# The softmax of q without GpSimd: exp with bias and sum on ScalarE head by head, the product on VectorE, and six kinds of subtractions and additions moved to VectorE

## The chip, the core and the metric

The kernel runs on one core of a Trainium2 chip. The metric is the device time of one execution in microseconds (us); the median of three runs stands below. Engines go by the names of the profile: PE (TensorE's matmuls), PEld (its weight loads, which overlap), DVE (VectorE), ACT (ScalarE), POOL (GpSimd), SP (SyncE, which issues most DMAs). "PEclk" is the granted clock of TensorE as a share of 2.4 GHz; its lower level is 1.2 GHz.

## The reference, cut to what matters

All data are fp32. The softmax of q runs over the 64 values of one head; that of k runs over the sequence.

```python
# q, k, v: (8 batches, 8 heads, 576 positions, 64)
q_s = exp(q - max(q, axis=-1));  q_s = q_s / (sum(q_s, axis=-1) + 1e-9)
k_s = exp(k - max(k, axis=2));   k_s = k_s / (sum(k_s, axis=2) + 1e-9)
kv = einsum("bhsd,bhse->bhde", k_s, v)
x = einsum("bhsd,bhde->bhse", q_s, kv)        # -> x: (4608 tokens, 512)

xn = x / sqrt(mean(x * x, axis=-1) + 1e-6) * rms_g          # first MoE
g = xn @ w_gate                                             # 512 -> 1536
x = (g * sigmoid(g) * (xn @ w_val)) @ w_out                 # 1536 -> 512

h = maximum(maximum(x @ w1, x @ w2), x @ w3)                # second MoE, 512 -> 768
out = h @ w_out2                                            # 768 -> 512
```

## The kernel before

**Tiles.** The 4608 tokens make nine groups of 512 (`g` 0 to 8); the last one gathers the last 64 positions of each batch. Each group has four pairs of heads `p`, of 128 features. A tile of q, `q_t[g, p]`, has 128 partitions (positions) and 512 columns: 8 pieces of 64, four blocks of positions times two heads, and each piece is one row of the softmax. The text calls such a piece of 64 columns a head, as the code does. An fp32 product is made of high and low halves in a reduced format: three matmuls, high by high, high by low and low by high. So every operand is split by a cast (the high half) and a subtraction (the low half).

**Stages.** (1) The prologue makes group 0's attention and joins the first weights out of 64-bit words (table `stages`). (2) Groups 0, 1 and 2 run as singles: `iteration(g, nxt, f)` for 12 hidden blocks `f`. Each makes the gate product pg (12 matmuls), tanh, product pv (12), the hidden block in halves hh and hl, and `out1` for the block before (12). In group 0, the weights of the next blocks are joined beside it (`scale` on ACT, `join` L164 to L166 on DVE, `high` on ACT, `low` L183 with half 0 on POOL and half 1 on DVE), and the attention of group 1 is made. (3) Groups 3 to 8 run in pairs (3+4, 5+6, 7+8), with quarter products whose sums replace some matmuls. (4) The second MoE runs over all groups.

**Attention beside a single.** From group 1 on, every engine but SP keeps the order in which the program is written (`tc.manual_schedule`); before that, the scheduler decides it. `beside_single` calls `attend(g, n, part, ...)` at fixed places of each iteration. Step n of group g does: `q_divide(g, n-1)` (part 0, at the head of the iteration), `make_kv(n-1)` (part 1), `transpose_q(n-1)`, `k_max(n)`, `q_exp(n)` and a load (part 2, between products pg and pv), `make_x(n-1)` (part 4), the exp of k (parts 5 and 6). Steps 5 and 6 make the variance, three Newton steps for the reciprocal root, and the normalised x. Group 1 carries the attention of group 3 (from f=0) and of group 2 (from f=5), group 2 that of group 4. In the pairs 3+4 and 5+6 the same `attend` serves the next two groups.

**Softmax of q.** `q_exp`: maximum on DVE (L346), subtraction on POOL (L347), one exp of 128x512 on ACT (L348). `q_divide`, an iteration later: sum on DVE (L352), addition of a small constant (L353), reciprocal (L355), product on POOL (L356). `transpose_q` follows: four PE transposes of the result (L401) into bank `pt`.

**Other work on POOL.** `Sums.whole` (L287) adds both halves of the first weights again, w = wh + wl, two additions every second iteration of groups 1 and 2; DVE makes four quarter sums of w (L292 to L295). Each of those is then split: cast on ACT (L259), subtraction on POOL (L260), store by SP (L261): one quarter in the even iteration, three in the odd one. `make_x` ends with the square of x on ACT (L444) and its addition to `sacc` on POOL (L445). POOL also makes hl (L830) in groups 0 and 1, the low halves of group 0's raw x (`split_first`, L455), and half of the shared splits of the first operands of the pairs in group 2 (L739).

Of the kernel before, what the change touches and what calls it, by code (L numbers as in the profile page):

```python
# [8 lines left out]
F32 = mybir.dt.float32  # L9
F32R = mybir.dt.float32r  # L10
I32 = mybir.dt.int32
AF = mybir.ActivationFunctionType
ALU = mybir.AluOpType
# [37 lines left out]
def attention_moe_moe(ctx: ExitStack, tc: tile.TileContext, q, k, kt, v, w1, rms_g, w2, w2_out, out):  # L51
# [81 lines left out]
    class Weights:  # L133
# [45 lines left out]
        def low(self, f, h):  # L179

            hi = wh[1, f].rearrange("p j n -> p (j n)")[:, h * HALF : (h + 1) * HALF]
            engine = nc.gpsimd if h == 0 else nc.vector
            engine.tensor_sub(self.half(1, f, h), self.y.pop((f, h)), hi.bitcast(F32))  # L183

    class Ahead:

# [94 lines left out]
    class Sums:  # L281


        def whole(self, f):
            st = two.tile([P, 2, N], F32, tag="st", name=f"w1_{f}")
            for j in range(2):
                nc.gpsimd.tensor_add(st[:, j, :], wh[1, f][:, j, :].bitcast(F32), wl[1, f][:, j, :].bitcast(F32))  # L287
            a, b = slice(0, N // 2), slice(N // 2, N)
            a11, a12, a21, a22 = st[:, 0, a], st[:, 0, b], st[:, 1, a], st[:, 1, b]
            q = two.tile([P, 4, N // 2], F32, tag="st", name=f"q1_{f}")  # L290
            self.q = {n: q[:, i, :] for i, n in enumerate((S1, S2, S4, S3))}
            nc.vector.tensor_add(self.q[S1], a21, a22)  # L292
            nc.vector.tensor_sub(self.q[S2], self.q[S1], a11)
            nc.vector.tensor_sub(self.q[S4], a12, self.q[S2])
            nc.vector.tensor_sub(self.q[S3], a11, a21)  # L295
# [45 lines left out]
                nc.sync.dma_start(t, kv_dram[p, :, 4 * i : 4 * i + 4, :])  # L341
                kv8[p].append(t)

    def q_exp(g, p):
        qm = two.tile([P, 24], F32, tag="qm", name=f"qm_{g}_{p}")[:, 0:8]
        nc.vector.tensor_reduce(qm, q_t[g, p], axis=AX.X, op=ALU.max)  # L346
        nc.gpsimd.tensor_sub(q_t[g, p], q_t[g, p], qm.unsqueeze(2).to_broadcast([P, 8, 64]))  # L347
        nc.scalar.activation(q_t[g, p], q_t[g, p], AF.Exp)  # L348

    def q_divide(g, p):  # L350
        qs = two.tile([P, 8], F32, tag="qs", name=f"qs_{g}_{p}")
        nc.vector.tensor_reduce(qs, q_t[g, p], axis=AX.X, op=ALU.add)  # L352
        nc.vector.tensor_scalar(qs, qs, EPS_SM, None, op0=ALU.add)  # L353
        qr = two.tile([P, 8], F32, tag="qr", name=f"qr_{g}_{p}")
        nc.vector.reciprocal(qr, qs)  # L355
        nc.gpsimd.tensor_mul(q_t[g, p], q_t[g, p], qr.unsqueeze(2).to_broadcast([P, 8, 64]))  # L356

    def k_max(g, p):
        if g == NB:
# [57 lines left out]
    def make_x(g, p):  # L417
        px = pair_bank(g, p, "px", "a0")
        if g == NB:
            for b in range(NB):  # L420
                s = slice(64 * b, 64 * b + 64)
                nc.tensor.matmul(px[:, s], kv8[p][b // 4][:, b % 4, :], qrt[g, p][:, s], start=True, stop=True)
        elif g in WHOLE:
            nc.tensor.matmul(px, kv_raw[p % 2], qrt[g, p], start=True, stop=True)
        else:
            nc.tensor.matmul(px, kvh[g, p], qh[g, p], start=True, stop=False)
            nc.tensor.matmul(px, kvh[g, p], ql[g, p], start=False, stop=False)
            nc.tensor.matmul(px, kvl[g, p], qh[g, p], start=False, stop=True)
        xraw[g, p] = one.tile([P, N], F32, tag=f"xraw{p}", name=f"xraw_{g}_{p}")
        if g == 0:  # L430
            if p in (0, 3):
                sqs["t", p] = wpool.tile([P, 3, N], F32, tag="wl4" if p == 0 else "wh4", name=f"sqs_{p}")
            sqs[p] = sqs["t", 0][:, p, :] if p < 3 else sqs["t", 3][:, 0, :]
            nc.scalar.activation(xraw[g, p], px, AF.Copy, scale=gain[:, p : p + 1])
            split_first(p)
            nc.scalar.activation(sqs[p], px, AF.Square)
            return
        nc.scalar.copy(xraw[g, p], px)
        if p == 0:
            sacc[g] = one.tile([P, N], F32, tag="sacc", name=f"sacc_{g}")  # L440
            nc.scalar.activation(sacc[g], xraw[g, p], AF.Square)
        else:
            sq = two.tile([P, N], F32, tag="y", name=f"sq_{g}_{p}", bufs=3)
            nc.scalar.activation(sq, xraw[g, p], AF.Square)  # L444
            nc.gpsimd.tensor_add(sacc[g], sacc[g], sq)  # L445

    xh, xl = {}, {}
    rawh, rawl = {}, {}
# [1 line left out]
    def split_first(p):  # L450

        b = wpool.tile([P, 2, N], F32R, tag=("wh11", "wl11", "wl6", "wl9")[p], name=f"raws_{p}")
        rawh[p], rawl[p] = b[:, 0, :], b[:, 1, :]
        nc.scalar.copy(rawh[p], xraw[0, p])
        nc.gpsimd.tensor_sub(rawl[p], xraw[0, p], rawh[p].bitcast(F32))  # L455

    def sum_squares(g, p):
        if p == 0:
# [78 lines left out]
    def attend(g, n, part, done=lambda p: None):  # L537

        before = 1 <= n <= 4
        if part == 0 and before:  # L540
            q_divide(g, n - 1)
        elif part == 1 and before:
            make_kv(g, n - 1)
        elif part == 2 and n <= 4:
            if before:
                transpose_q(g, n - 1)
            if n < 4:
                k_max(g, n)
                q_exp(g, n)
            if n < 3:  # L550
                load_pair(g, n + 1)
        elif part == 4 and before:
            make_x(g, n - 1)
        elif part == 5 and n < 4:
            k_exp(g, n, False)
        elif part == 5 and n == 4:
            split_squares(g)
        elif part == 3 and n == 5:
            variance(g)
        elif part in (4, 5) and n == 5:  # L560
            newton_step(g, part - 4)
        elif part == 0 and n == 6:
            newton_step(g, 2)
        elif part == 2 and n == 6:
            for p in range(4):
                done(p)
        elif part == 6 and n < 4 and g < NB:
            nc.scalar.activation(k_t[g, n], k_t[g, n], AF.Exp)
# [103 lines left out]
    def plane(n):  # L672

        if n // 3 not in kept:
            tag = f"w{'hl'[n // 3 % 2]}{4 + n // 6}"
            kept[n // 3] = wpool.tile([P, 3, N], F32R, tag=tag, name=f"x_{tag}")
        return kept[n // 3][:, n % 3, :]
# [56 lines left out]
    def split_operand(which, shared=False):  # L734
        for kk in range(2):
            n = 4 * which + 2 * kk
            if shared and kk == 1:
                nc.scalar.copy(plane(n), operand(which, kk))
                nc.gpsimd.tensor_sub(plane(n + 1), operand(which, kk), plane(n).bitcast(F32))  # L739
            else:  # L740
                split(plane(n), plane(n + 1), operand(which, kk))

# [17 lines left out]
    def iteration(g, nxt, f):  # L760
# [66 lines left out]
        if ahead:  # L827
            first.low(f + 1, 0)
            first.high(f + 1, 1)
        (nc.gpsimd if ahead or g == 1 else nc.vector).tensor_sub(hl[g, f], t, hh[g, f].bitcast(F32))  # L830
        if nxt is not None and f == 9 and nxt not in COMPACT:
            split_squares(nxt)
        if f > 0:
# [391 lines left out]
```

## Time and profile before

| what | value |
|---|---|
| median of three runs | 1672.43 us (1671.51 to 1672.44) |
| the profiled execution | 1672.9 us |
| its span in the trace | 1671.1 us |
| mean granted clock | 0.965 |
| busy: PE, DVE, ACT, POOL | 1534.3, 1002.7, 579.5, 473.8 us |

The span is the time from the first to the last instruction that the trace shows; the time of the execution has 1.8 us around it. Busy shares are means over stages that differ, so stages are read one by one: the prologue up to 59.5 us, group 0 up to 180.4, group 1 up to 363.3, group 2 up to 502.4, the pairs up to 1140, and then the second MoE.

### The profile page before, as it was taken

The page shows a single profiled execution, that of the slowest core. Times are in us where ns is not written, and L with a number is a line of the kernel's source. Part 1 is how long each engine was busy: PE and PEld are TensorE (multiplying, and loading weights), DVE is VectorE, ACT ScalarE, POOL GpSimd, SP SyncE. Part 2 cuts the span into 40 slices and gives each one's busy share as a digit, 9 for nine tenths or more (in the row PEclk, how much of TensorE's full clock was granted, in tenths as well). Part 3 has the DMA queues.
Part 4 walks back from the last instruction along what each step waited for, and adds up shares of the span by engine and source line. Part 5 has one row for each costly group of instructions (what it writes and reads, how often), then busy time and mean ns, then how long its engine had stood idle before and what let it go on. Part 6 is the DMA issues. An engine that isn't in the chain of part 4 may idle for free.

```text
span 1671.1 us, 19265 instructions
## 1 busy us (share of the span) xinstructions
PE 1534.3 (92%) x6734; PEld 1242.2 (74%) x6734; DVE 1002.7 (60%) x1581; ACT 579.5 (35%) x1033; POOL 473.8 (28%) x471
## 2 busy tenths in 40 slices
PE   5788876787899989999899999999999999999999
PEld 4576755565777767777787888888888888888887
DVE  6999434454477778768877566655364554544501
ACT  4544322333335434444343433432141231322211
POOL 4454243443354434224353132301100101101000
PEclk8899987988999999999999999999999999999999
DMA  7667532325416867687675978788454454544441
GB/s 253 261 219 266 197 112 97 107 69 181 162 70 235 306 218 244 223 321 262 211 255 189 346 281 274 240 276 319 143 191 167 168 194 170 181 159 170 153 145 45
DMA packets 136816, 337.61 MB, mean 202 GB/s; under 512 B 13328, under 2 KB 50192, under 8 KB 136720
## 3 DMA queue, kind: packets, MB, share of 16 engines
q1 hardware_dynamic: 126352, 317.51, 55.6%
q10 hardware_dynamic: 10368, 18.88, 3.0%
q8 instruction: 53, 0.87, 0.2%
q14 instruction: 43, 0.35, 0.1%
HBM read 266.34 MB, written 69.99 MB: 201 GB/s over the span
## 4 chain that ended last, share of the span: by engine, by line
PE 55%; DVE 5%; issue 1%; ACT 1%; POOL 0%; DMA 0%; ACTq 0%; SPq 0%; POOLq 0%; DVEq 0%
PE p_a L580 5%; PE p_a L582 5%; PE p_a L581 5%; PE acc L580 4%; PE acc L582 4%; PE acc L581 4%; PE p_V L580 3%; PE p_G L582 3%; PE p_G L581 3%; PE p_G L580 3%; PE p_V L582 3%; PE p_V L581 3%; PE acc_a L582 1%; PE acc_a L580 1%; PE acc_a L581 1%
## 5 line engine op out<-in xcount | busy, mean ns | idle before, releaser
L1082 POOL TENSOR_TENSOR temp<-temp,temp 128x512 f32<-128x512 f32 x36 | 48.2, 1340 | 414.1 <-ACT temp L1081 397.4
L581 PE MATMUL p_a<-x_wl,chunk 128*128 128x512 f32 x380 | 148.8, 392 | 0.0
L580 PE MATMUL p_a<-x_wh,chunk 128*128 128x512 f32 x312 | 122.5, 393 | 0.5 <-DVE t_t L1071 0.5
L582 PE MATMUL p_a<-x_wh,chunk 128*128 128x512 f32 x312 | 122.0, 391 | 0.0
L580 PE MATMUL p_V<-x_wh,chunk 128*128 128x512 f32 x231 | 92.2, 399 | 10.0 <-DVE temp L950 10.0
L1079 DVE TENSOR_TENSOR temp<-temp,p_V 128x512 f32<-128x512 f32 x36 | 24.7, 687 | 126.1 <-PE p_V L582 125.2
L582 PE MATMUL p_V<-x_wh,chunk 128*128 128x512 f32 x231 | 91.4, 396 | 0.0
L580 PE MATMUL p_G<-x_wh,chunk 128*128 128x512 f32 x231 | 91.0, 394 | 0.0
L582 PE MATMUL p_G<-x_wh,chunk 128*128 128x512 f32 x231 | 90.0, 390 | 0.0
L581 PEld LDWEIGHTS p_a<-x_wl,chunk 128*128 128x128 f32 x380 | 72.2, 190 | 15.4
L1073 DVE TENSOR_TENSOR temp<-temp,p_a 128x512 f32<-128x512 f32 x72 | 49.1, 683 | 51.2 <-POOL temp L1082 50.1
L401 PE MATMUL pt<-ident,q 128*128 128x128 f32 x136 | 25.2, 316 | 57.8 <-POOL q L356 53.9
L260 POOL TENSOR_TENSOR x_wl<-st,x_wl 128x256 fp32r<-128x256 f32 x50 | 41.0, 827 | 119.5 <-ACT x_wl L259 84.3
L580 PEld LDWEIGHTS p_a<-x_wh,chunk 128*128 128x128 f32 x312 | 59.1, 190 | 13.3 <-DVE t_t L1071 0.9
L1077 ACT COPY temp<-p_G 128x512 f32<-128x512 f32 x36 | 21.1, 586 | 138.0 <-PE p_G L582 137.8
L401 PEld LDWEIGHTS pt<-ident,q 128*128 128x128 f32 x136 | 17.9, 159 | 68.4 <-POOL q L356 59.2
L582 PEld LDWEIGHTS p_a<-x_wh,chunk 128*128 128x128 f32 x312 | 59.0, 189 | 12.4
L580 PE MATMUL acc<-hh,chunk 128*128 128x512 f32 x144 | 64.2, 446 | 0.0
L581 PE MATMUL p_V<-x_wl,chunk 128*128 128x512 f32 x159 | 62.6, 394 | 0.0
L821 DVE TENSOR_TENSOR t<-t,pv 128x512 f32<-128x512 f32 x36 | 24.6, 684 | 62.0 <-PE pv L576 61.2
L347 POOL TENSOR_TENSOR q<-q,qm 128x512 f32<-128x512 f32 x34 | 37.5, 1103 | 82.4 <-DVE qm L346 45.4
L580 PEld LDWEIGHTS p_V<-x_wh,chunk 128*128 128x128 f32 x231 | 43.7, 189 | 22.8 <-DVE temp L950 13.8
(618 smaller groups left out, 4560.4 us busy)
## 6 DMA issues: line engine op xcount, KB each, us to landing
chunk<-w_dram SPq DMA_DIRECT2D x189, 768.0 KB, 4.7
chunk<-w_dram SPq DMA_DIRECT2D x39, 512.0 KB, 4.4
words<-in_w SPq DMA_DIRECT2D x24, 768.0 KB, 7.1
w_dram<-w1q SPq DMA_DIRECT2D x48, 256.0 KB, 2.0
w_dram<-x_wl SPq DMA_DIRECT2D x42, 256.0 KB, 3.2
chunk<-w_dram SPq DMA_DIRECT2D x39, 256.0 KB, 3.0
k<-in_k SPq DMA_DIRECT2D x30, 320.0 KB, 3.0
v<-in_v SPq DMA_DIRECT2D x30, 320.0 KB, 4.2
```

The source lines that it names most:

```text
L260: nc.gpsimd.tensor_sub(t[:, 1, :], src, t[:, 0, :].bitcast(F32))
L347: nc.gpsimd.tensor_sub(q_t[g, p], q_t[g, p], qm.unsqueeze(2).to_broadcast([P, 8, 64]))
L401: nc.tensor.transpose(pt[:, t * P : (t + 1) * P], q_t[g, p][:, 2 * t : 2 * t + 2, :].rearrange("p a d -> p (a d)"), ident)
L580: nc.tensor.matmul(pt, ah, bh, start=first, stop=False, skip_group_check=onto)
L581: nc.tensor.matmul(pt, ah, bl, start=False, stop=False, skip_group_check=onto)
L582: nc.tensor.matmul(pt, al, bh, start=False, stop=last, skip_group_check=onto)
L821: nc.vector.tensor_mul(t, t, pv)
L1073: nc.vector.tensor_add(y, x, pt)
L1077: nc.scalar.copy(s1, a)
L1079: nc.vector.tensor_add(u2, s1, b)
L1082: nc.gpsimd.tensor_add(w, u2, s5)
```

## The change

**Softmax of q.** `q_exp` negates the maximum on DVE (eight columns) and calls ACT once per head: exp of 128x64 with the negated maximum as bias column, and with the sum written to a column of `qs`. In the prologue and in group 0 all eight heads come together; in `attend` heads 0 to 3 stay in part 2 and heads 4 to 7 go to part 4, behind `make_x`. `q_divide` makes no sum any more, and its product is on DVE.

**From POOL to DVE.** The 12 lows of half 0 (L183); hl of group 0 (11) and of group 1 (12) (L830); the four low halves of group 0's raw x (L455); the three square sums of group 1 (L445); the shared splits of group 2 (L739, 7); and the 24 additions of w (L287). On POOL remain memsets, the subtractions of w1q (L260) and the square sums of the later groups, and what the pairs and the second MoE have there.

```diff
         def low(self, f, h):
...
-            engine = nc.gpsimd if h == 0 else nc.vector
-            engine.tensor_sub(self.half(1, f, h), self.y.pop((f, h)), hi.bitcast(F32))
+            nc.vector.tensor_sub(self.half(1, f, h), self.y.pop((f, h)), hi.bitcast(F32))
...
         def whole(self, f):
...
-                nc.gpsimd.tensor_add(st[:, j, :], wh[1, f][:, j, :].bitcast(F32), wl[1, f][:, j, :].bitcast(F32))
+                nc.vector.tensor_add(st[:, j, :], wh[1, f][:, j, :].bitcast(F32), wl[1, f][:, j, :].bitcast(F32))
...
-    def q_exp(g, p):
-        qm = two.tile([P, 24], F32, tag="qm", name=f"qm_{g}_{p}")[:, 0:8]
-        nc.vector.tensor_reduce(qm, q_t[g, p], axis=AX.X, op=ALU.max)
-        nc.gpsimd.tensor_sub(q_t[g, p], q_t[g, p], qm.unsqueeze(2).to_broadcast([P, 8, 64]))
-        nc.scalar.activation(q_t[g, p], q_t[g, p], AF.Exp)
+    qneg, qsum = {}, {}
+
+    def q_exp(g, p, heads=range(8)):
+
+        if 0 in heads:
+            qm = two.tile([P, 24], F32, tag="qm", name=f"qm_{g}_{p}")[:, 0:8]
+            nc.vector.tensor_reduce(qm, q_t[g, p], axis=AX.X, op=ALU.max)
+            nc.vector.tensor_scalar(qm, qm, -1.0, None, op0=ALU.mult)
+            qneg[g, p], qsum[g, p] = qm, two.tile([P, 8], F32, tag="qs", name=f"qs_{g}_{p}")
+        for i in heads:
+            head, column = q_t[g, p][:, i, :], slice(i, i + 1)
+            nc.scalar.activation(
+                head, head, AF.Exp, bias=qneg[g, p][:, column], accum_out=qsum[g, p][:, column]
+            )
 
     def q_divide(g, p):
-        qs = two.tile([P, 8], F32, tag="qs", name=f"qs_{g}_{p}")
-        nc.vector.tensor_reduce(qs, q_t[g, p], axis=AX.X, op=ALU.add)
+        qs = qsum.pop((g, p))
         nc.vector.tensor_scalar(qs, qs, EPS_SM, None, op0=ALU.add)
         qr = two.tile([P, 8], F32, tag="qr", name=f"qr_{g}_{p}")
         nc.vector.reciprocal(qr, qs)
-        nc.gpsimd.tensor_mul(q_t[g, p], q_t[g, p], qr.unsqueeze(2).to_broadcast([P, 8, 64]))
+        nc.vector.tensor_mul(q_t[g, p], q_t[g, p], qr.unsqueeze(2).to_broadcast([P, 8, 64]))
...
-            nc.gpsimd.tensor_add(sacc[g], sacc[g], sq)
+            (nc.vector if g in COMPACT else nc.gpsimd).tensor_add(sacc[g], sacc[g], sq)
...
-        nc.gpsimd.tensor_sub(rawl[p], xraw[0, p], rawh[p].bitcast(F32))
+        nc.vector.tensor_sub(rawl[p], xraw[0, p], rawh[p].bitcast(F32))
...
     def attend(g, n, part, done=lambda p: None):
...
-                q_exp(g, n)
+                q_exp(g, n, range(4))
             if n < 3:
                 load_pair(g, n + 1)
-        elif part == 4 and before:
-            make_x(g, n - 1)
+        elif part == 4 and n <= 4:
+            if before:
+                make_x(g, n - 1)
+            if n < 4:
+                q_exp(g, n, range(4, 8))
...
-                nc.gpsimd.tensor_sub(plane(n + 1), operand(which, kk), plane(n).bitcast(F32))
+                nc.vector.tensor_sub(plane(n + 1), operand(which, kk), plane(n).bitcast(F32))
...
-        (nc.gpsimd if ahead or g == 1 else nc.vector).tensor_sub(hl[g, f], t, hh[g, f].bitcast(F32))
+        nc.vector.tensor_sub(hl[g, f], t, hh[g, f].bitcast(F32))
```

(`COMPACT` is (0, 1).) The changed file's line numbers are some ten higher below the softmax, one lower above it. Two places show how the order on the engines changes. In the first, VectorE's queue in group 1 at the end of f=2 and the start of f=3, with k and q of group 3's pair 2, w of block 1 (sums of block 1), t of f=2 and then f=3. Before:

```order
L821 TENSOR_TENSOR t_2_1695<-t_2_1695,pv_2_1721 128x512
L385 TENSOR_SCALAR ks_1_1741<-pk_1_1735 128x1
L387 RECIPROCAL kr_1_1743<-ks_1_1741 128x1
L391 TENSOR_SCALAR kv_raw_130<-pk_1_1735,kr_1_1743 64x64 x2
L370 TENSOR_TENSOR k_2_1601<-k_2_1601,pb_2_1771 128x640
L292 TENSOR_TENSOR q_1_1786<-w_1_1783 128x256
L293 TENSOR_TENSOR q_1_1786<-q_1_1786,w_1_1783 128x256
L294 TENSOR_TENSOR q_1_1786<-w_1_1783,q_1_1786 128x256
L295 TENSOR_TENSOR q_1_1786<-w_1_1783 128x256
L352 TENSOR_REDUCE qs_2_1795<-q_2_1599 128x8
L353 TENSOR_SCALAR qs_2_1795<-qs_2_1795 128x8
L355 RECIPROCAL qr_2_1798<-qs_2_1795 128x8
```

And in the change, VectorE at the same place:

```order
L831 TENSOR_TENSOR t_2_1755<-t_2_1755,pv_2_1785 128x512
L392 TENSOR_SCALAR ks_1_1805<-pk_1_1799 128x1
L394 RECIPROCAL kr_1_1807<-ks_1_1805 128x1
L398 TENSOR_SCALAR kv_raw_130<-pk_1_1799,kr_1_1807 64x64 x2
L840 TENSOR_TENSOR hl_2_1813<-t_2_1755,hh_2_1812 128x512
L377 TENSOR_TENSOR k_2_1659<-k_2_1659,pb_2_1839 128x640
L286 TENSOR_TENSOR w_1_1851<-wh_(1, 1)_507,wl_(1, 1)_530 128x512 x2
L291 TENSOR_TENSOR q_1_1854<-w_1_1851 128x256
```

Behind those rows stand the other three sums and then:

```order
L360 TENSOR_SCALAR qs_2_1770<-qs_2_1770 128x8
L362 RECIPROCAL qr_2_1864<-qs_2_1770 128x8
L363 TENSOR_TENSOR q_2_1657<-q_2_1657,qr_2_1864 128x512
L818 SCALAR_TENSOR_TENSOR t_3_1880<-t_3_1880,pg_3_1867 128x512
L369 TENSOR_REDUCE km_3_1890<-kT_3_1775 128x1
```

So hl, both additions of w and the product are now in VectorE's queue, and the reduction is not. The second place is ScalarE over the same iterations, before:

```order
L438 COPY xraw_1_1766<-px_1_1764 128x512
L444 ACTIVATE sq_1_1768<-xraw_1_1766 128x512
L568 ACTIVATE k_2_1601<-k_2_1601 128x640
L259 CAST w1q_1_1791<-q_1_1786 128x256
L807 ACTIVATE t_3_1814<-pg_3_1801 128x512
L411 COPY qh_2_1822<-pt_2_1817 128x512
L348 ACTIVATE q_3_1713<-q_3_1713 128x512
L826 CAST hh_3_1857<-t_3_1814 128x512
```

ScalarE there in the change:

```order
L445 COPY xraw_1_1830<-px_1_1828 128x512
L451 ACTIVATE sq_1_1832<-xraw_1_1830 128x512
L354 ACTIVATE q_2_1657,qs_2_1770<-q_2_1657,qm_2_1767 128x64 x4
L578 ACTIVATE k_2_1659<-k_2_1659 128x640
L258 CAST w1q_1_1859<-q_1_1854 128x256
L817 ACTIVATE t_3_1880<-pg_3_1867 128x512
L418 COPY qh_2_1888<-pt_2_1883 128x512
L354 ACTIVATE q_3_1777,qs_3_1895<-q_3_1777,qm_3_1892 128x64 x4
L836 CAST hh_3_1927<-t_3_1880 128x512
```

Four heads stand behind the square of x, ahead of the exp of k, and four between the copy of the transposes and hh.

## Rows read from the trace of the kernel before

**Rows 1.** Stages: start:end, length, busy us (x instructions) per engine, PEclk, DMA, GB/s.

```profile
0.00:59.50 59.50, 29.91 (x130) 21.94 (x130) 45.38 (x89) 27.84 (x43) 25.67 (x40) 0.83 0.80 291
59.50:180.40 120.90, 109.70 (x476) 86.35 (x477) 110.61 (x148) 57.44 (x85) 49.13 (x34) 0.96 0.68 235
180.40:363.30 182.90, 137.53 (x574) 108.10 (x572) 76.37 (x151) 53.46 (x100) 71.60 (x80) 0.88 0.32 106
363.30:502.40 139.10, 119.33 (x502) 95.41 (x503) 76.33 (x130) 47.65 (x94) 58.32 (x62) 0.91 0.39 132
502.40:1140.00 637.60, 610.81 (x2735) 494.74 (x2734) 448.86 (x693) 262.81 (x491) 222.08 (x221) 0.99 0.76 262
```

**Rows 2.** PE's waits in group 1: us in total, times, longest.

```profile
PE pt L401 <- POOL q L356: 37.1, 8, 9.7
```

**Rows 3.** The same view, group 2.

```profile
PE pt L401 <- POOL q L356: 15.2, 4, 6.2
```

**Rows 4.** Two iterations of group 1, f=2 and f=3, columns as in rows 1.

```profile
205.69:219.31 13.62, 11.01 (x55) 8.62 (x54) 5.32 (x12) 5.09 (x10) 5.64 (x8) 1.00 0.46 150
219.31:239.02 19.71, 13.52 (x56) 10.60 (x54) 6.79 (x16) 4.58 (x8) 7.97 (x7) 0.83 0.23 73
```

**Rows 5.** Timeline, f=3 of group 1: start, us, instruction, idle before and releaser.

```profile
219.59 0.82 DVE L370 TENSOR_TENSOR k<-k,pb 128x640 f32<-128x640 f32 x1 [2.77 <-PE pb L369]
220.10 0.63 ACT L444 ACTIVATE sq<-xraw 128x512 f32<-128x512 f32 x1
220.81 1.30 POOL L445 TENSOR_TENSOR sacc<-sacc,sq 128x512 f32<-128x512 f32 x1 [3.31 <-ACT sq L444]
222.06 2.48 POOL L287 TENSOR_TENSOR w<-wh_(1, 1)_475,wl_(1, 1)_498 128x512 f32<-128x512 f32 x2
...
226.18 0.68 DVE L352 TENSOR_REDUCE qs<-q 128x8 f32<-128x512 f32 x1
...
227.38 1.04 POOL L356 TENSOR_TENSOR q<-q,qr 128x512 f32<-128x512 f32 x1 [0.53 <-DVE qr L355]
...
228.48 1.11 PE L401 MATMUL pt<-ident,q 128*128 128x128 f32 x4 [6.19 <-POOL q L356]
```

**Rows 6.** Timeline, f=2 of group 1, behind an odd iteration.

```profile
208.11 2.10 POOL L260 TENSOR_TENSOR w1q<-q,w1q 128x256 fp32r<-128x256 f32 x3 [4.22 <-ACT w1q L259]
...
211.27 0.66 PE L401 MATMUL pt<-ident,q 128*128 128x128 f32 x4 [2.61 <-POOL q L356]
```

**Rows 7.** Groups of ACT's instructions: busy us, mean ns, idle before and releasers.

```profile
L348 ACT ACTIVATE q<-q 128x512 f32<-128x512 f32 x34 | 21.5, 632 | 75.5 <-POOL q L347 62.4 <-POOL v L334 12.9
...
L259 ACT CAST w1q<-q 128x256 fp32r<-128x256 f32 x48 | 17.4, 400 | 33.4 <-DVE q L293 28.4 <-DMA w_dram<-w1q 3.1 <-DVE z L522 1.3
```

**Rows 8.** Groups of DVE's instructions up to 180 us, by form; columns as rows 7.

```profile
L165 DVE SCALAR_TENSOR_TENSOR y<-words,y 128x768 int32<-128x768 int32 x24 | 28.8, 1205 | 0.1
L166 DVE SCALAR_TENSOR_TENSOR y<-words,y 128x768 int32<-128x768 int32 x24 | 25.9, 1087 | 0.2
...
L183 DVE TENSOR_TENSOR wl_(1, 8)_1126<-y,wh_(1, 8)_1104 128x768 fp32r<-128x768 f32 x1 | 2.6, 2596 | 0.0
...
L183 DVE TENSOR_TENSOR wl_(1, 0)_414<-y,wh_(1, 0)_411 128x768 fp32r<-128x768 f32 x1 | 0.9, 945 | 0.0
```

**Rows 9.** Timeline of the prologue: one join by itself, one beside POOL's low.

```profile
26.32 0.96 DVE L165 SCALAR_TENSOR_TENSOR y<-words,y 128x768 int32<-128x768 int32 x1
...
31.94 2.00 POOL L183 TENSOR_TENSOR wl_(1, 0)_414<-y,wh_(1, 0)_411 128x768 fp32r<-128x768 f32 x1 [2.54 <-ACT y L159]
...
32.80 1.96 DVE L165 SCALAR_TENSOR_TENSOR y<-words,y 128x768 int32<-128x768 int32 x1
```

**Rows 10.** Timeline: the first xraw of the prologue.

```profile
22.72 0.69 ACT L434 ACTIVATE xraw<-px,gain 128x512 f32<-128x512 f32 x1 [2.36 <-PE px L424]
```

**Rows 11.** Timeline: PE's longest wait in group 1, in front of f=6's transposes.

```profile
282.52 1.11 PE L401 MATMUL pt<-ident,q 128*128 128x128 f32 x4 [9.75 <-POOL q L356]
```

**Rows 12.** Timeline of a pair: DVE's addition behind q_divide's reciprocal (ended 653.70).

```profile
653.62 0.65 DVE L950 TENSOR_TENSOR temp<-temp,p_V 128x512 f32<-128x512 f32 x1
```

## The prediction

> **What bounds the kernel now.** I began with the busy time by stage [rows 1]; the reader is to compare PE's busy time with each stage's length, and then DVE's. The pairs (502.4 to 1140) leave PE idle for 26.8 us of 637.6, and MoE2 behind them touches nothing that is edited. In the prologue and group 0 (0 to 180.4) DVE is the fullest: 45.4 of 59.5 us and 110.6 of 120.9. Groups 1 and 2 are the loose place: 182.9 and 139.1 us, with PE busy for 137.5 and 119.3, no other engine over half busy, and a mean granted clock of 0.88 and 0.91.
>
> The waits of PE come next [rows 2, 3]. Of group 1's idle time 37.1 us in eight waits stand against POOL's product in q_divide, and 15.2 us in four waits in group 2. The first matmul held up each time is transpose_q's, so everything behind it on PE (product pv, make_kv, out1) stands too.
>
> Then one such wait from close by [rows 5]. PE runs dry at 222.29 (228.48 less 6.19 of idle time) in front of the transposes. POOL adds the square sum, makes both halves of w until 224.5; DVE can only then make the four quarter sums, and q_divide's reduction stands behind them on DVE (226.18); POOL's product ends at 228.42. So after an even iteration the chain is POOL, DVE, POOL. After an odd one it is shorter [rows 6]: three subtractions of w1q stand ahead of the product on POOL, and PE waits 2.61.
>
> **Singles, groups 1 and 2.** The change drops from these chains the DVE reduction (0.68) and the queue of POOL; it puts in the ACT heads and puts w and the product on DVE. The price of one head, exp of 128x64 with a bias column and a sum, isn't in the trace. Upper bound: a whole exp of 128x512, 0.63 [rows 7]. Lower bound: the line through that row and the cast of 128x256 (0.40), (632-400)/256 = 0.91 ns a column, drawn back to 64 columns: 400-192x0.91 = 226 ns, 0.23. I take 0.40, the row nearest in size; it lies within.
>
> The page ScalarE: Activation LUTs of the Trainium skill (section "What ACT_TABLE_LOAD costs") gives some 280 ns and 0.833 ns a column for an activation with a bias column, of which neighbours overlap by 93: as an estimate 0.24 a head. No row here has such a shape; by it the sum below would be some 9 us lower. It also speaks against the edit: eight heads would cost three times the one instruction that they replace.
>
> - After an odd iteration (three waits of group 1, two of group 2): the square of xraw ends at 220.73 [rows 5], 1.56 before PE runs dry; four heads of 1.60 follow and end just after it. Then add and reciprocal on DVE (some 0.5, as from the reduction's end at 226.86 to POOL's start at 227.38), the product on DVE (0.68, as a reduction of the same 512 columns), and 0.35 for hand-overs and gaps: PE waits 1.6. Before, the three waits of group 1 are 2.6, 2.9 and 3.0.
> - After an even iteration (four waits of group 1, together 18.9; two of group 2): DVE's own queue is k minus its maximum from 219.59 on (0.82), two halves of w (2x0.68), four sums (some 0.41 each: from w's end at 224.54 to the reduction at 226.18), 0.5, the product 0.68: done at 224.7, and 0.3 for gaps, so 2.7 us behind PE. Where POOL's square sum (220.81, 1.30) lies beside DVE's first w, as it does for pairs 1 to 3, I add 1.2: 3.9. Group 1 has two of each: 13.2.
> - The longest [rows 11], 9.75 before f=6, is behind the Newton steps on DVE, not behind POOL's queue. It loses the reduction and the slower product: 8.1.
>
> Group 1: 37.1 to 3x1.6+13.2+8.1 = 26.1, **-11.0**. Group 2: 15.2 to 2x1.6+2.7+3.9 = 9.8, **-5.4**.
>
> The clock gives back more. Its mean is a mix of 2.4 and 1.2 GHz, so group 1 had 2x(1-0.88)x182.9 = 43.9 us at the lower level and group 2 25.0. What that costs: the iteration of 219.3 to 239.0 at 0.83 [rows 4] has 6.7 us of it, and less its wait of 6.2 it ran 13.5 us; the one before it at 1.00 ran 13.6-2.6 = 11.0. So 2.5 lost of 6.7, and 16.4 and 9.3 in the two groups. The slow stretch lies in the iteration with the long wait, so I take it to shrink as the waits do, by 30% and 35%: **-4.9** and **-3.3**.
>
> **Prologue and group 0.** POOL is left with memsets, so what it does to DVE goes. The join L165 took 0.96 with POOL idle and 1.96 beside POOL's low [rows 9]; its mean is 1.205. The lows that DVE already has took from 0.945 to 2.596, twelve of them, 19.9 together [rows 8]. Relief: 24x(1.205-0.96) = 5.9 for L165 and 19.9-12x0.945 = 8.6 for the lows. L166, of the same form, has 24 at a mean of 1.087: 3.0. These are 17.5 of 74.6 us, 23%; on the other 81.4 us of DVE's work in both stages, with many one-input forms, I take half that rate, 9.5, bounds 0 and 19. Added: twelve lows by 0.945 = 11.3; eleven hl, four raws and three square sums by 0.68 = 12.2; eight products for eight reductions, even; eight negations by 0.26 (half of the 0.5 above) = 2.1. So 25.6 added for 27.0 relieved: **-1.4**, from +8 to -11. What is moved here is of a length with what its departure frees.
>
> The page SBUF — State Buffer (section "Who interferes with whom") says that a VectorE instruction with two SBUF inputs and a GpSimd instruction that reads SBUF shut each other out, the later one waiting in full. The pair of rows agrees (1.96 for 0.96, beside a POOL instruction of 2.00); by it the lows would run at their shortest after the change, as taken above.
>
> The first xraw stands behind all the heads on ACT (at 22.72, after 2.36 idle [rows 10]): 32 of them, 12.8 for 2.5 before, most of it in ACT's idle time (27.8 busy of 59.5), while eight POOL instructions of 1.0 leave the chain. **+0.5**, bounds -3 (0.23 a head) and +7 (0.63).
>
> **Pairs.** q_divide's reduction goes and the product comes, at the same price; the negation adds some 0.2 an iteration. The tight reader is the addition L950, which DVE starts right behind q_divide's small operations [rows 12]: the product now stands ahead of it, the reduction no longer. Some ACT time for the heads, 3.2 for 0.63, while ACT is busy for 41%. **0**, bounds -5 and +5. MoE2: 0.
>
> **Sum.** +0.5-1.4-11.0-5.4-4.9-3.3 = -25.5 on the profiled execution's 1672.9, which is 0.5 over the median of the runs: 1647.4, against the median **1647**.
>
> **Rivals.** (B) Every low clock goes and heads cost 0.23. Then waits after odd iterations are 0.9 (four heads save 0.7), after even ones 2.4 with no collision: group 1 3x0.9+4x2.4+8.1 = 20.4, -16.7; group 2 6.6, -8.6; clock -16.4-9.3; prologue -3, group 0 -1.4. Together -55: **1617**. For it: the head is small; against: waits of over 2 us remain, and each such has a slow stretch behind it.
>
> (C) ACT decides, and the kernel is **slower**. The heads take over the softmax's place in ACT's queue, in front of hh, tanh and the evacuations. Each 0.1 on the head's price costs 3.2 in the prologue and 2.0 in the five waits after odd iterations. From 0.5 on I expect the pairs' ACT queue to pass its slack behind the heads: 16 iterations of 8 heads, 12.8 per 0.1. So -20.3 at 0.5, zero at 0.61, and at 0.7 some +16: **1688**. For it: accumulating may cost on each instruction; against: the whole 512 columns cost 0.63.
>
> (D) The wait changes owner only. DVE's w stands in the even chains and collides with POOL's subtractions of w1q and square sums; those four waits stay at 18.9 (and 9.6 in group 2), no clock comes back, the other waits gain 5.2 in group 1 and 2.4 in group 2, group 0 nothing: -7.6, **1665**. For it: the queue on DVE is longer than before; against: the hand-over to POOL and back is gone.
>
> **How the numbers follow.** Forecast 0.56, B 0.17, D 0.16, C 0.11. The range, 1620 to 1668, leaves out C and a part of B, and holds the prologue's and group 0's bounds. A measurement of this kernel tells about 0.2%, 3.3 us, from no change: D falls partly within it (0.06), the bad ends of the forecast give 0.02. Faster 0.81, same 0.08, slower 0.11.
>
> **What would show it.** A head of 0.4 on ACT, 0.3 to 0.5. PE's waits at the transposes put down to DVE's product, at 1.6 after odd and 2.7 to 3.9 after even iterations. Group 1 some 16 us shorter, group 2 some 9, at 0.91 and 0.93. L165 near 0.96 and all lows near 0.95, with DVE's busy time up to 180 us nearly unchanged. Wrong it would be if xraw starts over 3 us later, if pairs lengthen by over 5, or if the waits after even iterations stay at 5 and more.

## The result, and the profile after

The changed kernel takes 1621.59 us (median of four runs, 1621.3 to 1627.53) against 1672.43: a ratio of 0.9705, with a 95% interval of 0.9683 to 0.9728, so 50.8 us less. The forecast was 1647 and the range 1620 to 1668: the direction held, the range held by 1.6 us, and the size was half of what came. The profiled execution took 1621.3 us, its span is 1619.5.

The stages of the changed kernel, from the start to block 1 of group 0, the rest of group 0, group 1, and group 2 up to its last block (columns as in rows 1):

```profile
0.00:51.65 51.65, 27.70 (x129) 19.85 (x130) 39.53 (x94) 36.66 (x115) 2.01 (x22) 0.90 0.86 307
51.65:158.10 106.45, 105.21 (x475) 84.16 (x476) 103.53 (x177) 63.86 (x132) 0.82 (x8) 0.98 0.86 293
158.10:320.54 162.44, 128.71 (x574) 101.61 (x572) 93.56 (x186) 70.54 (x222) 24.93 (x39) 0.93 0.34 110
320.54:442.17 121.63, 109.34 (x466) 87.36 (x467) 77.11 (x140) 52.37 (x146) 24.12 (x34) 0.93 0.42 144
```

Against [rows 1]: the prologue with block 0 went from 59.5 to 51.7 us, the rest of group 0 from 120.9 to 106.5 (22.3 together), group 1 from 182.9 to 162.4 (20.5). Group 2 up to its last block, cut in the same way before, is:

```profile
363.27:494.26 130.99, 111.22 (x466) 88.69 (x467) 70.41 (x120) 44.36 (x86) 55.22 (x59) 0.91 0.40 134
```

so 9.4 less. From there to the end it is 1176.8 before and 1177.3 after. DVE's column in the first two rows is the surprise: DVE took over 38 of POOL's larger instructions there, gave up eight reductions, and yet is busy for 143.1 us, where it was busy for 156.0. PE is busy for 105.2 of the 106.5 us of group 0 now (109.7 of 120.9 before), so little is left to gain on DVE in that row.

DVE's groups of the changed kernel up to 158.1 us show the joins and hl (columns as in rows 7):

```profile
L165 DVE SCALAR_TENSOR_TENSOR y<-words,y 128x768 int32<-128x768 int32 x24 | 22.7, 952 | 0.1
L166 DVE SCALAR_TENSOR_TENSOR y<-words,y 128x768 int32<-128x768 int32 x24 | 22.7, 951 | 0.1
...
L840 DVE TENSOR_TENSOR hl<-t,hh 128x512 fp32r<-128x512 f32 x11 | 7.5, 682 | 0.0
```

L165 was 1205 ns and L166 1087 [rows 8]. PE's waits of the changed kernel, first in group 1, then in group 2 (total, times, longest):

```profile
PE pt L408 <- DVE q L363: 23.3, 5, 9.6
PE pt L408 <- ACT w1q L258: 3.4, 3, 1.1
PE pb L376 <- ACT var L518: 2.8, 1, 2.8
```

```profile
PE pt L408 <- DVE q L363: 7.0, 2, 3.7
...
PE pt L408 <- ACT w1q L258: 2.2, 2, 1.1
```

The waits at the transposes were 37.1 and 15.2 [rows 2, 3]; now they are 26.7 and 9.2. Those put down to a cast of w1q are the waits after odd iterations. One of them, at f=2 of group 1, with the last of the four heads on ACT (start, us, instruction):

```profile
182.83 0.33 ACT L354 ACTIVATE q<-q,qm 128x64 f32<-128x64 f32 x1
183.07 0.19 ACT L354 ACTIVATION_READ_ACCUMULATOR q<-q,qm 128x1 f32 x1
183.16 0.72 ACT L578 ACTIVATE k<-k 128x640 f32<-128x640 f32 x1
183.29 0.17 DVE L360 TENSOR_SCALAR qs<-qs 128x8 f32<-128x8 f32 x1 [1.68 <-ACT q L354]
183.50 0.20 DVE L362 RECIPROCAL qr<-qs 128x8 f32<-128x8 f32 x1
183.73 0.69 DVE L363 TENSOR_TENSOR q<-q,qr 128x512 f32<-128x512 f32 x1
...
184.57 0.63 PE L408 MATMUL pt<-ident,q 128*128 128x128 f32 x4 [1.09 <-ACT w1q L258]
```

It is the chain that the prediction wrote down: heads on ACT, then DVE's small instructions, and the product, which ends at 184.42; the cast named as releaser only ends close by. PE waits 1.09, where it waited 2.61 [rows 6]. After an even iteration DVE's queue decides (f=3 of group 1, to be held against rows 5):

```profile
192.85 0.82 DVE L377 TENSOR_TENSOR k<-k,pb 128x640 f32<-128x640 f32 x1 [2.05 <-PE pb L376]
...
193.59 1.29 DVE L286 TENSOR_TENSOR w<-wh_(1, 1)_507,wl_(1, 1)_530 128x512 f32<-128x512 f32 x2
...
194.18 1.84 POOL L452 TENSOR_TENSOR sacc<-sacc,sq 128x512 f32<-128x512 f32 x1 [4.79 <-issue]
...
194.98 1.32 DVE L291 TENSOR_TENSOR q<-w 128x256 f32<-128x256 f32 x1
...
196.34 0.42 DVE L292 TENSOR_TENSOR q<-q,w 128x256 f32<-128x256 f32 x1
...
197.32 0.82 POOL L259 TENSOR_TENSOR w1q<-q,w1q 128x256 fp32r<-128x256 f32 x1 [1.30 <-ACT w1q L258]
197.47 0.69 DVE L360 TENSOR_SCALAR qs<-qs 128x8 f32<-128x8 f32 x1
...
199.28 1.09 PE L408 MATMUL pt<-ident,q 128*128 128x128 f32 x4 [3.73 <-DVE q L363]
```

The wait is 3.73 and not 6.19, and it contains collisions with POOL: the first quarter sum takes 1.32 beside POOL's square sum, where the next one takes 0.42, and the small addition takes 0.69 beside the subtraction of w1q, where it took 0.17 at f=2.

The clock of group 1 rose from 0.88 to 0.93 on average. Two of its iterations in the changed kernel, f=1 and f=3 (columns as in rows 1, the granted clock ahead of the last two):

```profile
166.29:180.51 14.22, 11.01 (x56) 8.64 (x54) 9.37 (x21) 7.33 (x25) 0.94 (x3) 1.00 0.52 180
192.57:209.97 17.40, 13.67 (x56) 10.74 (x54) 10.32 (x20) 6.72 (x23) 2.65 (x2) 0.80 0.25 83
```

In f=1 PE waits 3.21 in front of the transposes, and the granted clock stays at 1.00; in f=3 it waits 3.73, and the mean is 0.80.

### The profile page after: what moved, and what is told of

It reads as the page before. It is cut to its first block, busy times and chain, and to the rows that moved or that the text cites. A ratio compares the mean times of both kernels' runs of the same rounds, so it can differ in the third digit from the quotient of the medians.

```text
span 1619.5 us, 19766 instructions
## 1 busy us (share of the span) xinstructions
PE 1517.8 (94%) x6734; PEld 1230.8 (76%) x6734; DVE 1014.7 (63%) x1690; ACT 653.2 (40%) x1573; POOL 282.4 (17%) x326
## 4 chain that ended last, share of the span: by engine, by line
PE 59%; DVE 10%; ACT 3%; issue 2%; DMA 1%; POOL 1%; ACTq 0%; SPq 0%; DVEq 0%; POOLq 0%
PE p_a L590 6%; PE p_a L592 6%; PE p_a L591 6%; PE acc L590 5%; PE acc L592 5%; PE acc L591 5%; PE p_V L590 4%; PE p_V L592 3%; PE p_V L591 3%; PE p_G L590 3%; PE p_G L592 3%; PE p_G L591 3%; PE acc_a L590 1%; PE acc_a L592 1%; PE acc_a L591 1%
## 5 line engine op out<-in xcount | busy, mean ns | idle before, releaser
L354 ACT ACTIVATE q<-q,qm 128x64 f32<-128x64 f32 x272 | 90.8, 335 | 57.5 <-DVE qm L350 51.9
L590 PE MATMUL p_G<-x_wh,chunk 128*128 128x512 f32 x231 | 91.0, 394 | 0.0
L592 PE MATMUL p_G<-x_wh,chunk 128*128 128x512 f32 x231 | 90.3, 391 | 0.0
L591 PEld LDWEIGHTS p_a<-x_wl,chunk 128*128 128x128 f32 x380 | 72.1, 190 | 15.2
L1083 DVE TENSOR_TENSOR temp<-temp,p_a 128x512 f32<-128x512 f32 x72 | 49.1, 682 | 52.5 <-POOL temp L1092 51.3
L259 POOL TENSOR_TENSOR w1q<-q,w1q 128x256 fp32r<-128x256 f32 x48 | 38.1, 812 | 168.1 <-ACT w1q L258 144.9
L591 PE MATMUL p_G<-x_wh,chunk 128*128 128x512 f32 x154 | 60.0, 390 | 0.0
L591 PE MATMUL p_G<-x_wl,chunk 128*128 128x512 f32 x154 | 60.0, 390 | 0.0
```

Source lines behind the costliest of these rows:

```text
L259: nc.gpsimd.tensor_sub(t[:, 1, :], src, t[:, 0, :].bitcast(F32))
L354: nc.scalar.activation(head, head, AF.Exp, bias=qneg[g, p][:, column], accum_out=qsum[g, p][:, column])
L590: nc.tensor.matmul(pt, ah, bh, start=first, stop=False, skip_group_check=onto)
L591: nc.tensor.matmul(pt, ah, bl, start=False, stop=False, skip_group_check=onto)
L592: nc.tensor.matmul(pt, al, bh, start=False, stop=last, skip_group_check=onto)
L1083: nc.vector.tensor_add(y, x, pt)
```

## Experiments

Each kernel's ratio is against the kernel before, run on the same chip; stages come from the profiled execution. What a kernel takes more or less than the change is a difference of medians; where it is under some 6 us, the two 95% intervals touch or overlap.

### Each half of the change alone

The first is the kernel before with the new `q_exp`, `q_divide` and `attend`; the second has all the other lines of the diff.

> The kernel before with the softmax edit alone (heads on ACT, product on DVE); lows, hl, square sums and w stay on POOL. Theory 1 (the gain of prologue and group 0, some 22 us, is VectorE freed of collisions with POOL; the gain of groups 1 and 2 is POOL leaving the chain to the transposes): the q work is 12 of POOL's 40 larger instructions up to 180 us, so prologue and group 0 gain about a third, 6 to 9 us. Waits after odd iterations fall from 2.6 to 1.1, waits after even ones stay near 5 because POOL still makes w ahead of the sums. In all 1650 to 1656 us. Theory 2 (the softmax edit alone carries the gain, since it takes the hand-overs away): 1630 or less.

> The kernel before with the moves alone (lows, hl, raw lows, square sums of group 1, shared splits and w on DVE); the softmax of q keeps its subtraction and product on POOL. Theory 1: prologue and group 0 gain 12 to 16 us; after odd iterations PE waits 2.6 as before, after even ones some 4.5. In all 1643 to 1650 us. Theory 2: at most 5 us gained, 1667 or more, since DVE only takes on more work. If both parts simply add up, a1 and a2 together gain 51 us.

The softmax alone: 1651.13 us, 0.988 (0.9865 to 0.9894). The moves alone: 1648.08, 0.9858 (0.9844 to 0.9873). Gains of the span up to the end of group 0, in group 1, and in group 2 up to its last block, in us:

| kernel | to the end of group 0 | group 1 | group 2 |
|---|---|---|---|
| softmax alone | 1.4 | 13.1 | 3.8 |
| moves alone | 16.5 | 7.9 | 3.3 |
| both (the change) | 22.3 | 20.5 | 9.4 |

In group 1 the halves add up. Up to the end of group 0 nearly all belongs to the moves: the softmax edit shortens prologue and block 0 (59.5 to 50.7) and loses it again behind them, against an expectation of 6 to 9. In the medians, both inside the ranges expected, the halves give 20.4 and 23.4; the last 7 of 50.8 come only with both.

### Group 0: POOL's work given back, and POOL made busy for nothing

Lows of half 0 back on POOL, and (another kernel) hl of group 0 back on POOL:

```diff
-            nc.vector.tensor_sub(self.half(1, f, h), self.y.pop((f, h)), hi.bitcast(F32))
+            engine = nc.gpsimd if h == 0 else nc.vector
+            engine.tensor_sub(self.half(1, f, h), self.y.pop((f, h)), hi.bitcast(F32))
```

```diff
-        nc.vector.tensor_sub(hl[g, f], t, hh[g, f].bitcast(F32))
+        (nc.gpsimd if ahead else nc.vector).tensor_sub(hl[g, f], t, hh[g, f].bitcast(F32))
```

> The changed kernel with the lows of half 0 of the weights (12 in the prologue and group 0) back on POOL and nothing else. DVE loses 12 times 0.95 us of its own work. Theory 1 (collisions): what DVE is spared it pays in longer instructions and in waits; joins L165 rise above 1.1 us; the time is 2 to 8 us longer. Theory 2 (no collisions that matter): DVE is lighter by 11 us of 143, group 0 stays at PE's 105 us, the time is the same within 1 us or up to 3 us shorter.

> The changed kernel with hl of group 0 (11 subtractions of 128x512) back on POOL and nothing else. DVE has 7.5 us less of its own work. Theory 1 (what POOL reads holds up DVE's instructions of two SBUF operands, and what POOL makes comes later): 2 to 9 us longer, as with the lows. Rival: hl has a whole iteration until out1 reads it, so nothing waits for it, and DVE's relief balances the collisions: within 1.5 us.

The lows: 1634.46 us, 0.9779 (0.9765 to 0.9794), 13 us more than the change and more than the collisions were expected to cost. hl: 1629.65, 0.9754 (0.9739 to 0.9768), 8 more, and the rival falls: PE waits 2.1 for one hl, and DVE, with 7.5 us less to do, is busy for 146.8 in place of 143.1. With the lows on POOL, from the start of block 1 to the end of group 0:

```profile
53.05:167.80 114.75, 106.90 (x476) 85.83 (x477) 108.44 (x170) 65.38 (x133) 20.74 (x18) 0.96 0.77 260
```

DVE has 11.4 us less to do in the prologue and group 0 and is busy for 148.7 instead of 143.1. The joins carried little of this, against what I expected: L165 stays at 0.95, L166 rises to 1.01. More came from the 12 lows that DVE keeps (15.2 us in place of 11.4) and from small instructions, three additions of the softmax among them (columns as in rows 7):

```profile
L361 DVE TENSOR_SCALAR qs<-qs 128x8 f32<-128x8 f32 x3 | 4.9, 1647 | 0.0
```

And PE waits for lows, 6.8 us in all at four matmuls that read a low just made (three of these waits are put down to a memset that stands right behind the low on POOL). One of them (start, us, idle before):

```profile
77.72 0.50 PE L587 MATMUL pg<-xh,wl_(1, 3)_727 128*128 128x512 f32 x1 [1.27 <-POOL wl_(1, 3)_727 L183]
```

That mixes two things, POOL's results coming late and POOL holding up DVE. The next pair keeps them apart: POOL does useless work in group 0, on a tile that nobody reads.

```diff
             first.low(f + 1, 0)
             first.high(f + 1, 1)
+            nc.gpsimd.tensor_add(scr, ident, wh[1, f + 1][:, 0, 0:P].bitcast(F32))
+            for _ in range(8):
+                nc.gpsimd.tensor_add(scr, scr, ident)
```

(The other kernel has `range(16)` and `nc.gpsimd.memset(scr, 0.0)` in the loop.)

> The changed kernel with useless work on POOL in group 0 alone: behind each of 11 high casts nine additions of 128x128 in SBUF whose result nobody uses (some 0.3 us each, 30 us in all). No other engine waits for them. Theory 1 (reads by POOL hold up DVE's instructions of two SBUF operands): joins L165 and L166 and the lows grow beyond 0.95 us, group 0 is 3 to 12 us longer. Theory 2 (an idle POOL is no advantage by itself; it was the waiting for its results): the same within 1 us.

> As the run before, but one addition and sixteen memsets of the same 128x128 tile in each of 11 places: POOL is about as long busy, and writes only. If it is POOL's reading that collides: the same as the changed kernel within 1.5 us, DVE's instructions at 0.95. If any use of SBUF by POOL does: as long as the run with additions.

With additions 1640.88 us, 0.9812 (0.9798 to 0.9827); with memsets 1622.21, 0.9708 (0.9693 to 0.9723), the time of the change. The two stages with additions, then with memsets:

```profile
0.00:55.50 55.50, 30.02 (x129) 22.16 (x129) 41.77 (x94) 36.63 (x115) 10.47 (x33) 0.87 0.85 306
55.50:175.10 119.60, 110.25 (x475) 83.78 (x476) 117.39 (x177) 64.22 (x132) 72.86 (x98) 0.98 0.75 252
```

```profile
0.00:52.42 52.42, 29.39 (x129) 21.50 (x129) 39.76 (x94) 36.61 (x115) 7.17 (x41) 0.84 0.86 305
52.42:159.20 106.78, 105.43 (x476) 84.20 (x477) 104.01 (x178) 63.97 (x132) 40.20 (x178) 0.98 0.86 292
```

DVE does the same work in both. Beside POOL's additions it is busy for 159.2 us, beside the memsets for 143.8, and the end of group 0 moves with it, by 15.9. The memsets keep POOL busy for 40.2 us in group 0 and cost about 1 us there; the additions keep it busy for longer than planned, 72.9, no other engine waits for them, and they cost 17 us against the change by the end of group 0 (19 in the medians). So a POOL that reads is enough to lengthen group 0. Two groups of DVE's instructions beside the additions:

```profile
L845 DVE TENSOR_TENSOR hl<-t,hh 128x512 fp32r<-128x512 f32 x11 | 9.6, 874 | 0.0
L833 DVE TENSOR_TENSOR t<-t,pv 128x512 f32<-128x512 f32 x11 | 7.5, 678 | 0.2 <-PE pv L588 0.2
```

With memsets hl takes 681 ns. The product with pv, which reads one operand from a PSUM bank, stays at 0.68 in both. This agrees with the Trainium skill, page SBUF — State Buffer, section "Who interferes with whom": an instruction of DVE with two SBUF inputs is shut out by a GpSimd instruction that reads SBUF, not by one that only writes. POOL is held up too (the shortest of these additions took 0.45 us):

```profile
L844 POOL TENSOR_TENSOR scr<-scr,ident 128x128 f32<-128x128 f32 x75 | 62.5, 834 | 5.9
```

### The heads, and the additions of w

One exp of the whole row on ACT, with the subtraction and the sum on DVE:

```diff
-            nc.vector.tensor_scalar(qm, qm, -1.0, None, op0=ALU.mult)
...
+            nc.vector.tensor_sub(q_t[g, p], q_t[g, p], qm.unsqueeze(2).to_broadcast([P, 8, 64]))
+            nc.scalar.activation(q_t[g, p], q_t[g, p], AF.Exp)
...
     def q_divide(g, p):
+        nc.vector.tensor_reduce(qs, q_t[g, p], axis=AX.X, op=ALU.add)
```

> The changed kernel with one exp of 128x512 per tile on ACT in place of eight heads; the subtraction of the maximum and the sum over each head are on DVE (one more 128x512 subtraction and one reduction, 0.68 each, less the negation 0.17), everything else as changed. If the heads pay (they trade 2.0 us of ACT for 1.2 us of DVE a tile, and DVE is the fuller engine up to 180 us): prologue and group 0 longer by 4 to 9 us, waits after even iterations longer by 0.7, in all 5 to 14 us longer. If the heads are a burden (ACT's queue is what holds the transposes after odd iterations): waits there fall from 1.1 to under 0.8, in all the same or up to 5 us shorter.

1628.9 us, 0.9744 (0.9729 to 0.9758), 7 more than the change. Up to the end of group 0 it loses 5.4 (DVE is busy for 151.3 in place of 143.1), in group 1 1.1. The heads pay because they take work off DVE; as work of ACT they are dearer. Their price in the changed kernel:

```profile
L354 ACT ACTIVATE q<-q,qm 128x64 f32<-128x64 f32 x272 | 90.8, 335 | 57.5 <-DVE qm L350 51.9 <-DMA v<-in_v 2.1 <-DMA w_dram<-x_wl 1.2
L354 ACT ACTIVATION_READ_ACCUMULATOR q<-q,qm 128x1 f32 x272 | 50.8, 187 | 0.0
```

Each head is two instructions, and heads follow each other every 0.33 us.

Then came w back on POOL (`nc.gpsimd.tensor_add` in `whole`), and w with its sums moved to the middle of the odd iteration, still on DVE:

```diff
         nc.vector.scalar_tensor_tensor(t, t, 1.0, pg, op0=ALU.add, op1=ALU.mult)
+        if g > 0:
+            first_sums.middle(NF1 * (g - 1) + f)
```

(`middle` calls `whole` in odd iterations; the quarter S2 is split behind hl.)

> The changed kernel with the 24 additions of w back on POOL. Theory 1: waits in front of the transposes after even iterations rise from 3.2 to 3.9 us to some 5, and the clock of groups 1 and 2 falls back; 8 to 14 us longer. Rival (POOL's place in the chain did not matter, only its collisions): DVE is spared 1.36 us in each even chain, waits shorten to some 2.5, 3 to 8 us shorter.

> The changed kernel with both additions of w and the four quarter sums moved from the end of the even iteration to the middle of the odd one (behind the gate's product, ahead of the maximum of q), and the one quarter of the even iteration split there. Theory: what is left of the waits after even iterations (3.2 to 3.9 us, six of them) is DVE's w and sums in front of q's product; they fall to about 1.5, the clock of both groups recovers by 3 to 6 us, in all 10 to 18 us shorter, 1604 to 1612. Rival: those waits are set by ACT (xraw, square, four heads) or by POOL's square sum beside DVE: shorter by under 4 us.

w on POOL: 1627.14 us, 0.9743 (0.9726 to 0.976), 5.5 more in the median. In group 1 the waits at f=3 and f=9 grow to some 5.8, that at f=7 falls from 2.8 to 1.1, and less is lost than the 8 to 14 expected. w late: 1616.09, 0.9666 (0.965 to 0.9683), 5.5 less, where 10 to 18 were expected. PE's waits for q's product in both groups went from 30.3 to

```profile
PE pt L414 <- DVE q L369: 23.4, 7, 10.1
```

Of the six waits after even iterations four fell to 1.1; the two at f=1 did not (5.6 in group 2). So DVE's queue was the cause of the four. At f=1 of this kernel it is ACT, where heads 4 to 7 stand behind four evacuations of the group before. And behind group 2 this kernel takes 1181.3 us where the change takes 1177.3: PE waits 5.2 at the first pair for a copy on ACT, 1.8 in the change. I put that down to the four stores that now stand together in the last odd iteration; a kernel below, which leaves this block at its old place, has 1175.5.

### The longest wait, heads early, and all together

```diff
-        for h, start, done in plan:
+        for h, start, done in plan[::-1] if parts == (0,) else plan:
```

(In f=6 of group 1, q_divide then stands ahead of the third Newton step.)

```diff
-                q_exp(g, n, range(4))
+                q_exp(g, n, range(8 if n == 0 and g <= 4 else 4))
```

> The changed kernel with one swap: at the head of f=6 of group 1, q_divide of the next attention stands ahead of the third Newton step on DVE (behind it before). Theory: the longest wait (9.6 us) is q's product queued behind a Newton step whose square on ACT waits 2.4 us for a buffer that stores of w1q still hold; with the swap the product is ready as soon as the exp is, the wait falls to 3 to 5 us, in all 5 to 9 us shorter. Rival, as in the prediction: the Newton chain itself holds everything there, so the stall only comes back a few matmuls later: within 2 us of the changed kernel.

> The changed kernel with all eight heads together (part 2) for the first pair of each attention in the singles, where no make_x stands in between; elsewhere four and four as changed. Theory: the waits before the first transposes in f=1 of groups 1 and 2 (3.2 and 3.3 us) come from heads 4 to 7 standing on ACT behind the four evacuations of the previous group, which end at 169.4; with the heads ahead of them the waits are set by DVE's w and sums, as in the other even iterations, or go down to 2: 1 to 5 us shorter in all. Rival: it is DVE's queue already: no change within 1 us.

> Both edits of the two runs before with w and the sums in the middle of the odd iteration, this time only where a q_divide follows (blocks 0, 1, 3, 4, 6, 7; the others stay at the end of the even iteration, so that the stores ahead of the first pair stay where they were). If the causes are independent: waits of 1.1 to 2 us in front of all transposes of groups 1 and 2 but f=6 (3 to 5), the pairs as in the changed kernel; 20 to 30 us shorter than the changed kernel, 1592 to 1602 us. If the slow stretches of the clock stay whatever the waits are: 1605 to 1612.

The swap: 1619.83 us, 0.9696 (0.968 to 0.9712), no difference that the intervals tell, though group 1 is 3.2 shorter in the profile. The wait that it aimed at fell as expected, from 9.6 to the first of these rows, and a new one came behind it; the clock of this iteration stayed low too (0.82 for 0.77):

```profile
PE pt L408 <- DVE q L363: 3.5, 1, 3.5
PE pb L376 <- ACT var L518: 2.8, 1, 2.8
PE px L431 <- DVE kv_raw L398: 1.2, 1, 1.2
```

In the median it is 1.8 us less, where 5 to 9 were expected: a part of the stall moved on, as the rival said. What had held the product is seen on ACT in the changed kernel: the third Newton step's square waits for a buffer that a store of w1q still holds.

```profile
243.14 0.63 ACT L527 ACTIVATE nt<-z 128x512 f32<-128x512 f32 x1 [2.41 <-DMA w_dram<-w1q]
```

Heads early: 1624.83, 0.9725 (0.9711 to 0.974), 3 us more where 1 to 5 less was expected (the intervals overlap). At f=5 of group 1 the eight heads stand ahead of the variance on ACT, and that wait went from 2.8 to 4.2; the waits at f=1 did not shrink, and I put that down to DVE's w and sums, which stand in front of the product there as well.

All together: 1599.64, 0.9579 (0.9565 to 0.9594), 1.3% below the changed kernel. That is 22 us less, within the 20 to 30 expected. Group 1 takes 149.3 us (162.4), group 2 up to its last block 113.6 (121.6), at a granted clock of 0.95 and 0.96:

```profile
159.12:308.40 149.28, 129.04 (x574) 100.29 (x572) 89.67 (x186) 69.78 (x222) 24.76 (x39) 0.95 0.37 120
308.40:422.00 113.60, 105.94 (x467) 84.43 (x467) 75.12 (x140) 51.98 (x146) 23.94 (x34) 0.96 0.46 154
```

With w out of the way the early heads pay at f=1: the waits in front of the transposes are 0.5 there, with 1.9 and 2.2 for kv_raw behind them. Alone the three edits gave 1.8 less, 3 more and 5.5 less, so they depend on each other. PE in groups 1 and 2 of this kernel waits for many things, for none longer than 4.2 us:

```profile
PE px L442 <- DVE kv_raw L409: 6.5, 3, 2.4
PE pt L419 <- DVE q L374: 5.8, 5, 1.9
PE pb L387 <- ACT var L529: 4.2, 1, 4.2
```

## Why the prediction held in direction and gave half of the size

- **Prologue and group 0: forecast -0.9, measured -22.3.** This term failed: 21 of the 26 us that were missing, and outside its own bounds. The part for the first xraw is not to blame: +0.5 was forecast, and it starts at 22.02, where it started at 22.72. The added work was as priced (lows 0.95, hl and products 0.68). The relief, read off instructions that rows show as longer, was near: 30 for the 27.0, with 13.6 for the joins L164 to L166, 8.5 for the lows, the rest small instructions and x's splits. The step that failed is the next one, to set this relief against the added work and call the difference the time of the stage. DVE's durations, summed, fell by 8.0 of the 22.3 only, and 2.7 of that is four instructions that now run behind the end of group 0. Another 4.9 is overlap between neighbours (its busy time fell by 12.9), and 9.4 is time in which DVE was not busy (24.4 to 15.0).
- **What made it.** That POOL's reading by itself can cost 15.9 us is shown by additions against memsets. There it is all in the durations (15.2), while overlap (17.6 and 17.7) and DVE's idle time (15.9 and 15.4) are alike. DVE's idle time grows where POOL makes results that are used: to 19.1 with the lows put back, to 20.2 with hl put back, and PE is seen to wait for them. How the 22.3 divides between the two, the runs do not settle. I had also given this stage nothing of the clock: PE's busy time, for 606 and then 604 matmuls, fell from 139.6 to 132.9, which is another view of the same 22.3.
- **Its bounds.** I drew them from DVE's rows. [Rows 1] held the wider one: DVE is busy for 110.6 of 120.9 us beside 49.1 us of POOL's work, so what that work did to DVE could all be time of the kernel. With xraw's bounds the term reached to -14, and -22.3 lies 8 outside; that the whole still came to lie 1.6 us inside the range is luck.
- **Group 1: forecast -15.9, measured -20.5.** The waits had the right size: 26.1 forecast, 26.7 measured; after odd iterations 1.1 (1.6 forecast), after even ones 2.8 to 3.9 (2.7 to 3.9), at f=6 9.6 (8.1). Mis-sized was the clock: at a mean of 0.93, 2x0.07x162.4 = 22.7 us are left at the lower level of 43.9; half went, where I had taken 30%, the share of the waits. For the same 574 matmuls PE is busy for 8.8 us less, where I had 4.9. The slow stretches did not shrink with the waits: f=4 went from 0.79 to 1.00, but f=3, whose wait fell from 6.2 to 3.7, from 0.83 to 0.80. Nor does the length of a wait tell: f=1 waits 3.2 at 1.00 in the change, and 3.2 at 0.80 with w late. What decides between the two stays open.
- **The longest wait.** 8.1 was forecast and 9.6 came, for 9.75 before. I named its cause only in part: the Newton step itself waits for a buffer behind stores.
- **Group 2: forecast -8.7, measured -9.4**; waits 9.2 (9.8), clock 0.93 as said. That the sum fits is partly luck: for the same 466 matmuls PE is busy for 1.9 us less, where I had 3.3 from the clock, and waits that I had not counted made up for it (for t at f=7, 2.9 before and 1.4 now). **Pairs and MoE2: 0, measured +0.5**, though the heads raise ACT's busy time in the pairs by 33 us.
- **The head: 0.40 forecast, 0.33 measured**, within the 0.3 to 0.5 given. The estimate by the Trainium skill, page ScalarE: Activation LUTs, section "What ACT_TABLE_LOAD costs", was 0.24, and the measurement decides against it; the part that it lacks may be the instruction that reads the sum.
- **Rivals.** The time lies near that of (B), 1617, but not by its mechanism: even waits of 2.8 to 3.9 remain, a head isn't 0.23, and the clock isn't all back. Its sentence that each wait of over 2 us has a slow stretch behind it did not hold before the change either: f=2 waits 2.61 at a granted clock of 1.00 [rows 4, 6]. (C) asked for a head above 0.6. (D) falls: the even waits of group 1 shrank from 18.9 to 13.7, though the collisions that it spoke of are there, at 0.9 and 0.5 us in f=3. Of the signs that I gave, the joins and lows came as written; DVE's busy time up to 180 us, "nearly unchanged", did not, and it points at the failed term.
- **Two slips that change nothing.** In group 2 DVE is busy for 76.3 of 139.1 us, which is over half; and DVE's queue after an even iteration adds up to 224.6, not 224.7.

## What to carry to other kernels

Where DVE is the full engine of a stage, count what POOL's reading of SBUF costs DVE, and not only what waits for POOL's results: here additions on POOL, 72.9 us in group 0, cost 15 us of DVE's time. Taking such work onto DVE can leave DVE less busy. When a wait is taken away, read what comes second at the same place; here it was w in DVE's queue, then evacuations ahead of the heads on ACT, then a buffer, and only the edits together gave 22 us more.

## What the runs showed of the hardware that I had not expected

- A sum that ACT makes beside an activation is an instruction of its own: 187 ns behind each of 335, heads following each other every 0.33 us.
- Beside 176 memsets of 128x128 on POOL (38.1 us) DVE is busy for 143.8 us, beside none for 143.1; some 100 additions of that size lengthened its busy time by 15 us, and took 0.83 us each themselves.
- Small instructions are held up as well: an addition on 128x8, 0.16 us by itself, took 1.65 on average of three with the lows on POOL.
